# Output stage of a fused recurrence and soft-MoE kernel: eight one-bank PSUM places for both output engines become two one-bank places for ScalarE and three two-bank places for VectorE

## The chip, the cores and the metric

The kernel runs on one core of one Trainium2 chip. The metric is device time in microseconds of one launch; the time before is the median of three runs. A profile is one further execution of the same program, recorded by the hardware profiler. Engines are named as the profile names them: PE is TensorE (PEld its weight loads), DVE is VectorE, ACT is ScalarE, POOL is GpSimd, SP is SyncE, which here issues the output's DMAs.

## The reference, cut to what matters

```python
B, S, D = 4, 5056, 256          # batch, tokens, channels
E, SPE, F = 8, 4, 1024          # experts, slots per expert, hidden size; 32 slots in all

# 1. a gated recurrence along the tokens of each batch
sig = 1 / (1 + exp(-f_logit));  f = lb + (1 - lb) * sig;  i = 1 - f
h[t] = f[t] * h[t-1] + i[t] * x[t]                  # x: [20224, 256] afterwards

# 2. a soft mixture of experts over all 20224 tokens
logits = x @ phi                                    # [20224, 32]
d = softmax(logits, over tokens);  slot_input = d.T @ x     # [32, 256]
slot_out = per expert: relu(slot_input @ w1) @ w2           # [32, 256]
c = softmax(logits, over slots)
out = c @ slot_out                                  # [20224, 256] float32, 20.7 MB
```

Only the last line, the output stage, is touched by the change. It can begin when slot_out is known, which needs all tokens and all experts.

## The kernel before, in words

The first 143 us read f_logit and x (41 MB), run the recurrence and the slot sums, and apply the experts. They leave in SBUF:

- `etall`: exp(logits) of all tokens, the 32 slots of sequence (batch entry) b on partitions 32 b to 32 b + 31;
- `rrow`: the reciprocal of the sum over slots for each token and sequence;
- `slot_out` (L750, VectorE): the experts' output, on the same partitions as `etall`, bf16;
- `slot_bd` (L759, GpSimd, two instructions): the same in two blocks of columns, zero where the sequence is of the other parity, so that one matmul with 64 rows makes the output of two sequences at once.

Just before the output stage, three rows of block 0 of the last sequence are made early: VectorE's L755 and ScalarE's L753 and L756 read `early_ps` out of PSUM, and SP issues them as `total` (L754) and `early` (L757).

The 5056 tokens of a sequence are cut into blocks: blocks 0 and 1 have 16 rows of 128 tokens, the short block (index `end` = 2) has 7 rows, and 64 left-over tokens remain. A row is one matmul into PSUM: 256 columns for one sequence alone (L776, in `share`), 512 columns for a pair of sequences (L828, in `couple`). A vector or scalar instruction then reads it out of PSUM, multiplies by `rrow` and writes the SBUF tile `ob` (one sequence) or `oc` (a pair): `by_vector` (L766) is one VectorE instruction, `by_scalar` (L770) one ScalarE instruction for each 256 columns. When a tile is full, SP issues its DMA: one for a sequence of a block, two for a pair (2 MB each for blocks 0 and 1, 896 KB each for the short block).

PSUM has eight banks of 512 float32 columns. The pool `pout` has eight places of one bank (`bank()`), used by both engines. `next_engine()` gives rows to ScalarE and VectorE in turn. The tile framework places the waits: a matmul into a place waits until the reader of what lay there before is done, and a tile in SBUF waits for the DMA that read its place. Each engine runs its instructions in the order of the program; the order is written out by hand in the last lines of the kernel:

1. `pieces(0, B - 1)`: the remaining 13 rows of block 0 of the last sequence, in five pieces of two to four rows, each with a DMA of its own (L802), VectorE and ScalarE taking a share of each piece;
2. `couple(end, 0)`, `couple(end, 1)`: the short block of all four sequences (L828, L834);
3. `rest()`: the left-over 64 tokens of all sequences, two matmuls (L843), ScalarE copies (L847), VectorE additions and one scaling (L848, L766), two DMAs (L851);
4. `whole(0, B - 2)`: block 0 of sequence 2 alone (L776, L819);
5. `couple(0, 0)`, `couple(1, 0)`, `couple(1, 1)`: what is left of blocks 0 and 1, six DMAs of 2 MB (L834).

Of the kernel before, what the change touches and what calls it, by code (L numbers as in the profile page):

```python
# [9 lines left out]
F32 = mybir.dt.float32  # L10
BF16 = mybir.dt.bfloat16
AX = mybir.AxisListType
ALU = mybir.AluOpType
ACT = mybir.ActivationFunctionType
PSUM = bass.MemoryType.PSUM
# [3 lines left out]
def kernel(  # L19
# [10 lines left out]
    nc = tc.nc  # L30
    B, S, D = x.shape
    E = moe_w1.shape[0]
    F = moe_w1.shape[2]
    NS = moe_phi.shape[1]
    SPE = NS // E
    P = 128
    DC = D // P
    FC = F // P
    R = 4
    G = P * R  # L40
    n_grp = (S + G - 1) // G
# [18 lines left out]
    wide_r = 4 * R  # L60
    n_blk = (S // (P * wide_r))
    blocks = [(i * P * wide_r, wide_r) for i in range(n_blk)]
# [57 lines left out]
    etall = store.tile([P, S + PAD], BF16, name="etall")[:, :S]  # L120
    rrow = store.tile([P, n_grp * R, B], F32, name="rrow")
# [6 lines left out]
    slot_bd = store.tile([P, 2, D], BF16, name="slot_bd")  # L128
# [39 lines left out]
    with tc.tile_pool(name="sp2", bufs=3) as sp2, \  # L168
# [85 lines left out]
        def to_channels(n, ps, t, rest):  # L254
            t = t.bitcast(F32)
            if n // B == odd:
                flat = ps.rearrange("c p r -> c (p r)")
                sides = ident_f.rearrange("p (t u) -> p u t", u=2)
                v = flat[:, ds(0, P * R3)].rearrange("c (p r) -> c p r", r=R3)
                k = P * R3 - n % 2 * L  # L260
                nc.tensor.matmul(flat[:, ds(k, P)], rest.bitcast(F32), sides,
                                 is_transpose=True, start=True, stop=True)
                for r in range(R3):
                    nc.tensor.transpose(v[:, :, r], t[:, r], ident_f)
                return
            for r in range(R):
                nc.tensor.transpose(ps[:, :, r], t[:, r], ident_f)  # L267
# [217 lines left out]
        for n in range(n_unit):  # L485
# [14 lines left out]
            else:  # L500
                end = n >= n_unit - 6
# [97 lines left out]
        for o in range(DC):  # L599
            nc.tensor.matmul(sin_ps[:, o], slot_v[:, o], rep[:, 0],  # L600
                             start=True, stop=True, skip_group_check=True)
# [3 lines left out]
    with tc.tile_pool(name="ew", bufs=1) as ew, \  # L605
# [18 lines left out]
        for q in range(E // Q):  # L624
            hi = ew.tile([P, F], BF16, name=f"hi{q}")
            for k in range(2):
                hi_ps = (psu.tile([P, H], F32, name="hi_ps", tag="up") if q == 0 else
                         pbig.tile([P, H], F32, name="hi_ps", tag=f"hi_ps{k}"))
                for o in range(DC):
                    for j in range(Q):  # L630
                        nc.tensor.matmul(hi_ps[ds(j * NS, NS)], sin[:, o],
                                         w1_sb[q * Q + j][:, o, ds(k * H, H)],
                                         start=(o == 0), stop=(o == DC - 1),
                                         skip_group_check=True)
# [7 lines left out]
        for q in range(E // Q):  # L642
# [4 lines left out]
            if q == 0:  # L647
                nc.tensor.matmul(cs_ps, rep2, cs1, start=True, stop=True)
            k = Q if q == 0 else Q - 1
# [4 lines left out]
            dst = hid[:, :, q * Q, ds(s0, SPE)]  # L654
            dst = bass.AP(tensor=dst.tensor, offset=dst.offset,
                          ap=[list(dst.ap[0]), [(E - 1) * NS, FC], [NS + SPE, k], [1, SPE]])
# [31 lines left out]
        for i in range(n_late):  # L688
# [3 lines left out]
                             start=True, stop=True, skip_group_check=True)  # L692
# [20 lines left out]
        q = n_grp * R - 1  # L713
        for i in range(len(blocks)):
            expert(Q + i)
            row_sums(i)
            if i < len(blocks) - 1:
                spin(so_ps, 3, D)
                k = ds(i * wide_r, wide_r)
# [3 lines left out]
        k = len(blocks) - 1  # L723
# [39 lines left out]
    with tc.tile_pool(name="osb", bufs=3, reuse_waits="tile") as osb:  # L763

        def by_vector(ob, op, scale):
            nc.vector.tensor_tensor(ob, op, scale.broadcast_to(list(ob.shape)), ALU.mult)  # L766

        def by_scalar(ob, op, scale):
            for i in range(ob.shape[1]):
                nc.scalar.activation(ob[:, i], op[:, i], ACT.Copy, scale=scale[:, i])  # L770

        def share(op, i, b, r, k):
            t0, n_r = blocks[i]
            ew = etall[ds(b * NS, NS), ds(t0, P * n_r)].rearrange("s (p r) -> s p r", r=n_r)
            for j in range(k):
                nc.tensor.matmul(op[:, j], ew[:, :, r + j], slot_out[ds(b * NS, NS)],  # L776
                                 start=True, stop=True, skip_group_check=True)

        def scale_of(i, b, r, k):
            return rrow[:, ds(blocks[i][0] // P + r, k), ds(b, 1)]  # L780

        def rows_of(i, b):
            t0, n_r = blocks[i]
            return out[ds(b * S + t0, P * n_r)].rearrange("(p r) d -> p r d", r=n_r)

        pout = ctx.enter_context(
            tc.tile_pool(name="pout", bufs=8, space=PSUM, reuse_waits="tile"))

        def bank():
            return pout.tile([P, 2, D], F32, name="op", tag="op")  # L790

        def pieces(i, b):
            dst = rows_of(i, b)
            ob = osb.tile([P, blocks[i][1], D], F32, name="ob", tag="ob")
            for r, ks in ((3, (1, 1)), (5, (1, 1)), (7, (1, 1)), (9, (2, 2)), (13, (2, 1))):
                q = r
                for k, by in zip(ks, (by_vector, by_scalar)):
                    op = bank()
                    share(op, i, b, q, k)
                    by(ob[:, ds(q, k)], op[:, ds(0, k)], scale_of(i, b, q, k))  # L800
                    q += k
                nc.sync.dma_start(out=dst[:, ds(r, q - r)], in_=ob[:, ds(r, q - r)])  # L802

        turn = [0]

        def next_engine():
            turn[0] += 1
            return turn[0] % 2

        def whole(i, b):  # L810
            n_r = blocks[i][1]
            ob = osb.tile([P, n_r, D], F32, name="ob", tag="ob")
            for r in range(0, n_r, 2):
                k = min(2, n_r - r)
                op = bank()
                share(op, i, b, r, k)
                (by_scalar, by_vector)[next_engine()](
                    ob[:, ds(r, k)], op[:, ds(0, k)], scale_of(i, b, r, k))
            nc.sync.dma_start(out=rows_of(i, b), in_=ob)  # L819

        def couple(i, j):
            t0, n_r = blocks[i]
            ew = etall[ds(j * 2 * NS, 2 * NS), ds(t0, P * n_r)].rearrange(
                "s (p r) -> s p r", r=n_r)
            ob = osb.tile([P, 2, n_r, D], F32, name="oc", tag="oc")
            for r in range(n_r):
                op = bank()
                nc.tensor.matmul(op.rearrange("p u d -> p (u d)"), ew[:, :, r],  # L828
                                 slot_bd[ds(j * 2 * NS, 2 * NS)].rearrange("s u d -> s (u d)"),
                                 start=True, stop=True, skip_group_check=True)  # L830
                (by_scalar, by_vector)[next_engine()](
                    ob[:, :, r], op, rrow[:, t0 // P + r, ds(2 * j, 2)].unsqueeze(2))
            for u in range(2):
                nc.sync.dma_start(out=rows_of(i, 2 * j + u), in_=ob[:, u])  # L834

        def rest():
            n_p = B // 2
            ob = osb.tile([P, n_p, D], F32, name="ob", tag="ob")
            dst = out.rearrange("(b t) d -> t b d", b=B)
            for j in range(n_p):  # L840
                k = ds(j * 2 * NS, 2 * NS)
                op = bank()
                nc.tensor.matmul(op.rearrange("p u d -> p (u d)"),  # L843
                                 left[k].rearrange("s t u -> s (t u)"),
                                 slot_bd[k].rearrange("s u d -> s (u d)"),
                                 start=True, stop=True, skip_group_check=True)
                nc.scalar.copy(ob[:, j], op[:, 0])  # L847
                nc.vector.tensor_tensor(ob[:, j], ob[:, j], op[:, 1], ALU.add)  # L848
            by_vector(ob, ob, rrow[:, n_grp * R - 1, ds(0, n_p)].unsqueeze(2))
            for j in range(n_p):  # L850
                nc.sync.dma_start(out=dst[ds(S - L, L), ds(2 * j, 2)], in_=ob[:, j])  # L851

        pieces(0, B - 1)
        end = len(blocks) - 1
        couple(end, 0)
        couple(end, 1)
        rest()
        whole(0, B - 2)
        for i in range(end):
            for j in range(B // 2):  # L860
                if i or j < B // 2 - 1:
                    couple(i, j)


# [28 lines left out]
```

## Time and profile before

| | us |
|---|---|
| median of 3 runs | 197.69 |
| lowest, highest | 197.34, 197.92 |
| profiled execution, its own time | 197.27 |
| its span, from the first to the last instruction | 195.5 |
| first matmul of the output stage (L776) | 143.47 |
| last PE instruction of the output stage ends | 172.3 |
| last ScalarE instruction ends | 173.6 |

| engine | busy us | share of the span |
|---|---|---|
| PE | 148.4 | 76% |
| DVE | 144.4 | 74% |
| ACT | 141.9 | 73% |
| POOL | 101.8 | 52% |

The span is shorter than the time by what lies around the program (1.8 us here). The shares are means over stages with different limits; the output stage is the last quarter of the span and is read by itself. In the timeline a line gives the start in us, how long the stretch of like instructions took, engine, line of the kernel, operation, what it writes and reads, how many, and in brackets the idle time before it and what ended that. A row like "128x512 f32<-128x512 f32" gives partitions and columns written and read.

### The profile page before, as it was taken

The page shows a single profiled execution, that of the slowest core. Times are in us where ns is not written, and L with a number is a line of the kernel's source. Part 1 is how long each engine was busy: PE and PEld are TensorE (multiplying, and loading weights), DVE is VectorE, ACT ScalarE, POOL GpSimd, SP SyncE. Part 2 cuts the span into 40 slices and gives each one's busy share as a digit, 9 for nine tenths or more (in the row PEclk, how much of TensorE's full clock was granted, in tenths as well). Part 3 has the DMA queues.
Part 4 walks back from the last instruction along what each step waited for, and adds up shares of the span by engine and source line. Part 5 has one row for each costly group of instructions (what it writes and reads, how often), then busy time and mean ns, then how long its engine had stood idle before and what let it go on. Part 6 is the DMA issues. An engine that isn't in the chain of part 4 may idle for free.

```text
span 195.5 us, 3277 instructions
## 1 busy us (share of the span) xinstructions
PE 148.4 (76%) x1202; PEld 104.3 (53%) x1202; DVE 144.4 (74%) x187; ACT 141.9 (73%) x200; POOL 101.8 (52%) x79
## 2 busy tenths in 40 slices
PE   0687599977998979899797987998888999920000
PEld 0476468675776767667585866556664334300000
DVE  2669759989699999999999999544287998920000
ACT  3588686899889999999987799434089999950000
POOL 2689578774998688874969979253030000000000
PEclk9999759996999999999999999999999555555555
DMA  6999999999999999999999999999949999999994
GB/s 212 421 417 417 438 427 419 421 427 370 371 427 426 408 333 419 424 416 335 378 420 422 252 215 214 213 215 214 164 182 417 424 431 429 426 429 429 433 433 211
DMA packets 14305, 70.75 MB, mean 362 GB/s; under 512 B 1601, under 2 KB 2882, under 8 KB 10322
## 3 DMA queue, kind: packets, MB, share of 16 engines
q1 hardware_dynamic: 11520, 62.13, 76.8%
q0 software_dynamic: 2768, 8.42, 21.7%
q8 instruction: 9, 0.15, 0.3%
q14 instruction: 6, 0.05, 0.1%
q10 hardware_dynamic: 2, 0.00, 0.0%
HBM read 58.23 MB, written 20.71 MB: 404 GB/s over the span
## 4 chain that ended last, share of the span: by engine, by line
PE 30%; DMA 20%; DVE 16%; POOL 9%; ACT 7%; issue 5%; SPq 1%; POOLq 1%; ACTq 0%; DVEq 0%
DVE h L319 12%; DMA w_t<-in_moe_w_dram 9%; PE op L828 8%; DMA x_t<-in_x_dram 7%; POOL u_t L252 7%; ACT oc L770 5%; PE hp L332 5%; PE sp L267 4%; PE up L273 4%; DMA f_t<-in_f_logit_dram 4%; DVE ht L351 3%; PE slot_ps L189 2%; PE lg L365 2%; POOL w_sb L147 2%; PE slot_ps L416 1%
## 5 line engine op out<-in xcount | busy, mean ns | idle before, releaser
L252 POOL TENSOR_TENSOR u_t<-s_t,x_t 128x1024 bf16<-128x1024 bf16 (+1 forms) x39 | 82.5, 2131 | 22.8 <-ACT s_t L241 11.9
L319 DVE TENSOR_TENSOR_SCAN h<-a,h,up 128x512 bf16<-128x512 f32 (+1 forms) x72 | 86.8, 1252 | 4.5 <-PE up L273 2.2
L241 ACT ACTIVATE s_t<-f_t 128x2048 bf16<-128x2048 f32 (+2 forms) x23 | 38.3, 1668 | 4.7 <-DMA f_t<-in_f_logit_dram 4.6
L332 PE MATMUL hp<-ident_f,h 128*128 128x128 f32 (+1 forms) x160 | 29.5, 309 | 8.0 <-DVE ht L351 6.7
L332 PEld LDWEIGHTS hp<-ident_f,h 128*128 128x128 f32 (+1 forms) x160 | 23.5, 207 | 19.1 <-DVE ht L351 12.7
L267 PE MATMUL sp<-ident_f,s_t 128*128 128x128 f32 x144 | 22.1, 299 | 6.7 <-ACT s_t L241 4.4
L301 ACT ACTIVATE a<-sp,lbs 128x1024 f32<-128x1024 bf16 x24 | 25.4, 1114 | 1.1 <-PE sp L267 1.0
L770 ACT ACTIVATE oc<-op,rrow 128x256 f32<-128x256 f32 x62 | 24.2, 525 | 0.1
L828 PE MATMUL op<-slot_bd,etall 64*128 64x512 bf16 x62 | 22.5, 570 | 0.7 <-POOL slot_bd L759 0.4
L267 PEld LDWEIGHTS sp<-ident_f,s_t 128*128 128x128 f32 x144 | 18.2, 155 | 8.5 <-ACT s_t L241 4.9
L308 ACT ACTIVATE a<-sp,lbs 128x512 f32<-128x512 bf16 (+2 forms) x22 | 17.8, 857 | 4.7 <-PE sp L267 4.4
L766 DVE TENSOR_TENSOR oc<-op,rrow 128x512 f32<-128x512 f32 x31 | 19.8, 683 | 1.6 <-PE op L828 1.6
L273 PE MATMUL up<-ident_f,u_t 64*128 64x64 f32 x192 | 17.7, 231 | 1.8 <-POOL u_t L252 1.8
L189 PE MATMUL slot_ps<-rep,ident_f 128*128 128x256 f32 x52 | 17.5, 432 | 0.0
L273 PEld LDWEIGHTS up<-ident_f,u_t 64*128 64x128 f32 x192 | 14.1, 139 | 5.6 <-POOL u_t L252 2.1
L828 PEld LDWEIGHTS <-etall 64*128 64x128 bf16 x62 | 9.1, 153 | 13.4 <-issue 8.2
L351 ACT COPY ht<-hp 128x512 f32<-128x512 f32 (+1 forms) x20 | 11.7, 583 | 5.5 <-PE hp L332 5.3
L351 DVE COPY ht<-hp 128x512 f32<-128x512 f32 (+1 forms) x20 | 13.4, 669 | 1.4 <-PE hp L332 1.4
L319 DVE TENSOR_TENSOR_SCAN h<-a,up 128x512 bf16<-128x512 f32 x8 | 9.3, 1208 | 2.6 <-ACT a L308 1.7
L365 PE MATMUL lg<-h,phi 128*32 128x512 bf16 (+1 forms) x80 | 9.8, 412 | 0.3 <-ACT et L389 0.2
L267 PE MATMUL up<-ident_f,u_t 128*128 128x128 f32 x48 | 9.4, 327 | 0.7 <-POOL u_t L252 0.7
L189 PEld LDWEIGHTS slot_ps<-rep,ident_f 128*128 128x128 f32 x52 | 8.5, 199 | 1.8 <-issue 0.8
(132 smaller groups left out, 144.9 us busy)
## 6 DMA issues: line engine op xcount, KB each, us to landing
f_t<-in_f_logit_dram SPq DMA_DIRECT2D x12, 1024.0 KB, 12.0
x_t<-in_x_dram SPq DMA_DIRECT2D x12, 1024.0 KB, 11.5
out_dram<-oc SPq DMA_DIRECT2D x6, 2048.0 KB, 13.7
w_sb<-in_moe_w_dram POOLq DMA_DIRECT2D x14, 512.0 KB, 10.2
f_t<-in_f_logit_dram SPq DMA_DIRECT2D x12, 512.0 KB, 8.4
x_t<-in_x_dram SPq DMA_DIRECT2D x12, 512.0 KB, 9.9
out_dram<-oc SPq DMA_DIRECT2D x4, 896.0 KB, 5.7
out_dram<-ob SPq DMA_DIRECT2D x1, 2048.0 KB, 9.2
```

Source lines behind the costliest of these rows:

```text
L189: nc.tensor.matmul(slot_bank[:, 1], ident_f, wide_rep, start=False, stop=False, skip_group_check=True)
L241: nc.scalar.activation(s_t, f_t, ACT.Sigmoid, scale=-1.0)
L252: nc.gpsimd.tensor_tensor(uts[n][:, :r], s_t[:, :r], x_t[:, :r], ALU.mult)
L267: nc.tensor.transpose(ps[:, :, r], t[:, r], ident_f)
L273: nc.tensor.transpose(v[:, :, r], t(r)[k].bitcast(F32), ident_f[k, k])
L301: nc.scalar.activation(a, sp[:, :, :, :, o], ACT.Identity, scale=nomlb[:, ds(o, 1)], bias=1.0)
L319: nc.vector.tensor_tensor_scan(h[:, :T, o], decays[n // 2, o][:, n % 2, :T], up[:, :T, o], hs[number(g - 1, b)][:, ds(used(g - 1) - 1, 1), ...
L332: nc.tensor.transpose(hp[:n_p, r], hw[:, :n_p, r], ident_f)
L351: copy(hts[g][:n_p, b].rearrange("p r d -> p (r d)").bitcast(F32), hps.pop(n)[:n_p].rearrange("p r c -> p (r c)"))
L766: nc.vector.tensor_tensor(ob, op, scale.broadcast_to(list(ob.shape)), ALU.mult)
L770: nc.scalar.activation(ob[:, i], op[:, i], ACT.Copy, scale=scale[:, i])
L828: nc.tensor.matmul(op.rearrange("p u d -> p (u d)"), ew[:, :, r], slot_bd[ds(j * 2 * NS, 2 * NS)].rearrange("s u d -> s (u d)"), start=Tru ...
```

## The change

The pool gets two kinds of places: `one()`, one bank, two of them, for ScalarE; and `two()`, two banks, three of them, for VectorE, whose instruction now covers up to 1024 columns (four rows of one sequence or two rows of a pair). One `two()` is taken at the start and not used, which shifts the turn of the three. A list of steps takes the place of the strict turn: in a block of 16 rows for a pair the steps are (1, 2, 2, 1, 2) twice, where a 1 is a ScalarE row and a 2 a VectorE instruction over two rows.

The short block's first pair of sequences is no longer made as a pair: `whole(end, 0)` and `whole(end, 1)` make them singly from `slot_out`. The second pair stays a pair. `rest()` is called after `whole(0, B - 2)`, not before it, and its scale is folded into its two kinds of instructions (L862 on ScalarE, L863 on VectorE), so that its third VectorE instruction goes. The line of `by_vector` and `by_scalar` stays L766 and L770, that of the single matmul L776; the pair's matmul is now L783, the pieces' DMA L820, the DMA of `whole` L828, that of `couple` L848, and those of `rest` L866.

```diff
         pout = ctx.enter_context(
-            tc.tile_pool(name="pout", bufs=8, space=PSUM, reuse_waits="tile"))
-        def bank():
-            return pout.tile([P, 2, D], F32, name="op", tag="op")
+            tc.tile_pool(name="pout", bufs=1, space=PSUM, reuse_waits="tile"))
+        def one():
+            return pout.tile([P, 2, D], F32, name="one", tag="one", bufs=2)
+        def two():
+            return pout.tile([P, 2, 2, D], F32, name="two", tag="two", bufs=3)
+        two()
+        def single(ob, i, b, r, k, vector):
+            if vector:
+                op = two().rearrange("p q u d -> p (q u) d")
+            else:
+                op = one()
+            matmuls(op, i, b, r, k)
+            (by_vector if vector else by_scalar)(
+                ob[:, ds(r, k)], op[:, ds(0, k)], scale_of(i, b, r, k))
...
+        def whole(i, b, steps):
+            ob = osb.tile([P, blocks[i][1], D], F32, name="ob", tag="ob")
+            r = 0
+            for k in steps:
+                single(ob, i, b, r, k, k > 2)
+                r += k
             nc.sync.dma_start(out=rows_of(i, b), in_=ob)
...
+            for k in steps:                                  # couple(i, j, steps)
+                scale = rrow[:, ds(t0 // P + r, k), ds(2 * j, 2)]
+                if k == 1:
+                    op = one()
+                    pair_matmul(op, i, j, r)
+                    by_scalar(ob[:, :, r], op, scale[:, 0].unsqueeze(2))
+                else:
+                    op = two()
+                    for q in range(k):
+                        pair_matmul(op[:, q], i, j, r + q)
+                    by_vector(ob[:, :, ds(r, k)].rearrange("p u r d -> p r u d"), op,
+                              scale.unsqueeze(3))
...
-                nc.scalar.copy(ob[:, j], op[:, 0])
-                nc.vector.tensor_tensor(ob[:, j], ob[:, j], op[:, 1], ALU.add)
-            by_vector(ob, ob, rrow[:, n_grp * R - 1, ds(0, n_p)].unsqueeze(2))
+                nc.scalar.activation(ob[:, j], op[:, 0], ACT.Copy, scale=scale)
+                nc.vector.scalar_tensor_tensor(ob[:, j], op[:, 1], scale, ob[:, j],
+                                               ALU.mult, ALU.add)
...
         pieces(0, B - 1)
-        couple(end, 0)
-        couple(end, 1)
+        whole(end, 0, (2, 4, 1))
+        whole(end, 1, (2, 4, 1))
+        couple(end, 1, (1, 2, 1, 2, 1))
+        whole(0, B - 2, (2, 4, 2, 4, 4))
         rest()
-        whole(0, B - 2)
         for i in range(end):
             for j in range(B // 2):
                 if i or j < B // 2 - 1:
-                    couple(i, j)
+                    couple(i, j, (1, 2, 2, 1, 2) * (wide_r // 8))
```

## The prediction

> **What bounds the kernel now.** I read the page first, then windows of the output stage (143 us to the end), then each engine's timeline there, then the DMA issues one by one. The chain of waits names PE L828 and ACT L770, but it starts from the last instruction of an engine, and engines stop at 173.7 us of 195.5. What runs after that is DMA.
>
> ```profile
> PEclk9999759996999999999999999999999555555555
> DMA  6999999999999999999999999999949999999994
> GB/s 212 421 417 417 438 427 419 421 427 370 371 427 426 408 333 419 424 416 335 378 420 422 252 215 214 213 215 214 164 182 417 424 431 429 426 429 429 433 433 211
> ```
>
> One slice is 4.9 us. From slice 31 the DMA engines stay at 9 and 417 to 433 GB/s: 20.7 MB are written between 144.0 and 193.7 us at an even rate, and 1.8 us of closing work follow. So the output stage is one full DMA queue, and an engine's time matters only if a transfer is issued so late that the queue runs dry. The issues:
>
> ```profile
> 143.88 0.34 SPq L757 DMA_DIRECT2D out_dram<-early  x1
> 144.39 2.58 SPq L802 DMA_DIRECT2D out_dram<-ob  x5
> 148.51 4.09 SPq L834 DMA_DIRECT2D out_dram<-oc  x4
> 153.13 2.17 SPq L851 DMA_DIRECT2D out_dram<-ob  x2
> 155.56 1.14 SPq L819 DMA_DIRECT2D out_dram<-ob  x1
> 160.62 14.30 SPq L834 DMA_DIRECT2D out_dram<-oc  x6
> ```
>
> How much room has each? Bytes first move at 144.0, 0.8 us after the first issue (L754 at 143.19); its 128 KB take 0.4 us and land 1.9 us after the issue, so a landing tells 0.5 to 0.7 us late (I take 0.5). A 2 MB transfer takes 4.9 us at 430 GB/s. The transfer of 155.56 lands 9.2 us later and the first of 160.62, couple(0,0)'s, 9.1 us later. The latter needs 0.8 + 4.9 + 0.5 = 6.2 us by itself, so it lay 2.9 us in the queue: the room before couple(0,0) is 2.9 us. In other words the queue would have been empty at 164.3, and an issue after 163.5 leaves it dry. The later couples have twice that room and more. At the front, 'early' (256 KB, 0.7 us at 390 GB/s) keeps the queue busy from 144.7 to 145.5, and the first piece, issued at 144.39, is ready at 145.2: room 0.3 us.
>
> What sets 160.62? These windows are 3.41 us long, on the grid of the clock's changes.
>
> ```profile
> 144.76:148.18 3.42, 2.85 (x15) 1.55 (x14) 3.42 (x7) 3.42 (x10) 0.67 (x1) 1.00 1.05 406
> 148.18:151.59 3.41, 2.65 (x17) 1.71 (x16) 2.06 (x4) 3.41 (x11) 0.00 (x0) 1.00 1.01 416
> 151.59:155.00 3.41, 3.11 (x11) 1.37 (x10) 3.34 (x7) 3.41 (x12) 0.00 (x0) 0.50 1.01 423
> 155.00:158.42 3.42, 3.42 (x9) 1.30 (x8) 3.42 (x7) 3.42 (x11) 0.00 (x0) 0.50 0.99 414
> ```
>
> Columns: PE, PEld, DVE, ACT, POOL busy, granted clock, DMA share, GB/s. TensorE loses half its clock at 151.59 and never regains it, though it is busy all the time. A couple's 512-column matmul then starts every 0.427 us (weight loads at 155.19, 155.61, 156.04), so 16 rows take 6.8 us. With eight banks PE is far ahead: it begins couple(0,0) at 153.04 (timeline), when VectorE begins whole(0,2).
>
> **The change part by part.** Pitches: VectorE 0.60 us for 512 columns (four take 2.48) and 0.335 for 256. For 1024 no row exists. Bounds: two separate 512s, 1.20, and twice the 256-to-512 step on top, 0.60 + 2 x 0.265 = 1.13; I take 1.13, since the step between the two rows is the cost of columns alone. ScalarE: 0.36 for 256 (14 in 5.22). A reader can begin 0.31 us after a full-clock 256-column matmul starts, 0.67 after a half-clock 512 one (160.73 to 161.40). A reader's end frees PE 0.05 later (143.42 to 143.47).
>
> *First place.* The first two-bank place lies on the banks of early_ps[1], which VectorE L755 reads until 143.81. In the built program the first matmul of pieces now waits for that L755, where before it waited for slot_out (L750, ended 143.42). So pieces moves by 0.39 us, from 143.47 to 143.86, and everything on all engines behind it. Of the room of 0.3 about 0.2 us is overdrawn: **+0.2 us**, bounds 0 and 0.4.
>
> *Two places for ScalarE.* The third piece's ScalarE matmul waits for ScalarE's first instruction to end. That costs about 0.1 us per piece, and SP's issues (0.4 to 0.5 us each) still come before the queue empties: nothing by itself, because piece 4's 512 KB and piece 5's 384 KB lie ahead of the short block.
>
> *Short block.* Its first transfer (896 KB) leaves after one sequence instead of after a pair, but at 148.65, not 148.51: PE waits for ScalarE's last piece (146.46), VectorE's 1024-column tile runs 147.40 to 148.54. Room at that point 0.4 us before and after. No gain, since the queue was full there already; no loss.
>
> *Left-over later, and its places.* This is the costly part. rest() now follows whole(0,2). Its two tiles are ScalarE places, read by VectorE too (L863), and VectorE executes in order: that instruction stands behind three 1024-column ones of whole(0,2). The next ScalarE place, couple(0,0)'s first row, waits for it in the built program (VectorE's signal 157, the first L863). Behind that matmul on PE stand all other matmuls. So PE, which before was 2.4 us ahead, stops, VectorE then runs out of tiles, and couple(0,0) begins with empty places.
>
> The schedule, clock half from 148.2 (reasoned below): pieces end 146.6 on VectorE; first sequence's tile ends 148.5; second 150.1; end pair 153.1; whole(0,2) three tiles, 153.7 to 157.2; first L863 ends 157.67 (0.35 + 0.1 for its end). PE then starts couple(0,0) at 157.7, 16 x 0.427 = 6.83, ends at 164.55. The last tile's second matmul starts at 164.12, VectorE begins 0.67 later, 164.8, and ends 1.2 later: issue at about 166.1, against 160.62. The last tile holds both sequences, so the first transfer can't go one instruction ahead as before.
>
> The queue is empty at 164.3 + 0.2 = 164.5; bytes of couple(0,0) come at 166.1 + 0.8 = 166.9: **dry for 2.5 us**. Behind it couple(1,0) comes at 173, room 3 us. So the loss stays and does not grow. Sum at this clock: 0.2 + 2.5 = 2.7, upper with 1.20 a tile 3.2.
>
> *The clock.* In 144.76 to 148.18, which kept the clock, PE ran 12 matmuls of 64 rows x 512 and 2 of 32 x 256. In 148.18 to 151.59, which lost it, 4 of the former and 12 of the latter: 229 thousand row-columns against 410 thousand. After the change the window from 144.76 holds only single sequences, some 19 of 32 x 256, 156 thousand. So the clock should fall one window earlier, near 148.2; where the grid lies in another run is unknown, and any window inside 143.9 to 149.5 has singles alone, so 146.2 to 149.6. By the same schedule this gives +3.3 (146.2) to +2.2 (149.6). I take the middle of the last two, **+2.5**.
>
> The Trainium skill speaks of this in TensorE: Matmul & The Clock Gate, section Part 1: The HAM clock gate: the clock is halved after an idle window of about 3.4 us and is whole again after one busy window. The trace disagrees on both: it fell after a window with PE busy 2.65 of 3.41 us and stayed half through one busy 3.42 of 3.42. By the page's rule couple(0,0) would run at the whole clock, which is a rival below. The page's section A second HAM failure mode: psum-queue depth-cycling says that cycling PSUM banks with short PE pauses degrades matmul throughput; that speaks against this change, and here its price is the early fall.
>
> *Fewer, longer instructions; L862/L863 with the scale folded in.* ScalarE's load falls, VectorE's rises to 6 x 1.13 = 6.8 us per couple, about PE's 6.83. Later couples therefore stay as fast as before and have room. Cover: the DMA queue. If it went, a couple would still cost PE's 6.8.
>
> **Rivals.**
> (a) *Not slower: the room holds.* If VectorE never waited for PE after pieces (ready at 146.6), its work until couple(0,0) is done is 13 x 1.13 + 2 x 0.35 = 15.4, to 162.0: issue before 163.5, and only the 0.2 of the front is lost: 197.9. For it: PE had spare time until 151. Against it: PE's wait on L863 is in the program, and the half clock.
> (b) *Clock whole.* Matmuls every 0.215: the schedule gives couple(0,0) at 164.1, dry 0.6, total +0.8: 198.5. For it: the page's rule. Against it: the rows above.
> (c) *Clock falls at 151.6 as before.* PE starts couple(0,0) at 156.6, issue 165.0, dry 1.4, total +1.6: 199.3.
> (d) *Faster*, the short block fed earlier. The DMA moves bytes from 144.0 to 193.7 without a hole over 0.2 us, so at most the hole at 144.5 and some hand-overs could go, -0.6: 197.1. The same bytes in the same packets speak against it.
>
> **How the numbers follow.** The profiled execution took 197.27 us (span 195.5, 1.8 around it); the median is 197.69, 0.4 above. I add to the median: 197.7 + 2.5 = 200.2. Chances: forecast with its earlier and later falls 0.50; (c) 0.18; (b) 0.14; (a) 0.13; (d) 0.05. A difference under 0.3% (0.6 us) is about what a measurement of this kernel can't tell from none. Slower: 0.50 + 0.18 + 0.14 = 0.82; same 0.13; faster 0.05. The range runs from 197.9, (a), to 201.5 (a fall at 144.8, or 146.2 with 1.20 a tile, +3.8).
>
> **What would show it.** The first L776 at about 143.86, released by DVE early; PEclk half from about 148; an idle PE before couple(0,0)'s first matmul, ended by the first L863, then idle VectorE; the first 2 MB issue of couple(0,0) near 166 with about 6.2 us to landing instead of 9.1; a DMA hole of 2 to 3 us near 165. It is wrong if that transfer is issued before 163.5 or the DMA row shows no hole.

## The result, and the profile after

| | before | after |
|---|---|---|
| median, us | 197.68 | 200.51 |
| lowest, highest | 197.34, 197.92 | 200.16, 200.72 |
| profiled execution, its own time | 197.27 | 200.63 |
| its span | 195.5 | 198.9 |
| last byte of the output moved (trace of the DMA engines) | 193.68 | 197.12 |

Four runs each. The ratio after to before is 1.0143, with a 95% interval from 1.0121 to 1.0164: the change costs 2.8 us. The forecast was 200.2, range 197.9 to 201.5.

Three rows of the page of the changed kernel, in 40 slices of 4.97 us: the granted clock, the DMA engines' busy share, and what they moved.

```profile
PEclk9999889997999999999999999999965555555555
DMA  6999999999999999999999999999499994999996
GB/s 213 416 421 421 433 422 422 425 433 338 404 420 422 380 360 437 422 405 308 409 420 366 234 213 214 213 214 210 71 357 409 435 395 169 448 425 422 422 422 264
```

The output stage, from slice 30 to the end, now has a slice at 169 GB/s and share 4 (number 34, 164 to 169 us) between full ones. Packet by packet, nothing moves from 164.71 to 167.75 us: a hole of 3.04 us. Behind it the queue is as full as before. The hole, a smaller one of 0.09 at 150.14 and a later start (below) make up the 3.44 us by which the last byte is late.

SP's queue in the timeline of the changed kernel (start, length, line, transfer, how many):

```profile
144.03 0.57 SPq L757 DMA_DIRECT2D out_dram<-early  x1
144.93 2.50 SPq L820 DMA_DIRECT2D out_dram<-ob  x5
149.39 1.84 SPq L828 DMA_DIRECT2D out_dram<-ob  x2
153.81 0.84 SPq L848 DMA_DIRECT2D out_dram<-oc  x2
...
166.90 15.22 SPq L848 DMA_DIRECT2D out_dram<-oc  x6
```

couple(0,0)'s first 2 MB leave at 166.90, 6.3 us later than before, and land 6.3 us after the issue, with no time spent in a queue. Why it leaves so late is seen on PE and VectorE. The timeline of PE in the changed kernel, from whole(0,2) on:

```profile
154.57 1.91 PE L776 MATMUL two<-slot_out,etall 32*128 32x256 bf16 x8
156.41 0.61 PE L858 MATMUL one<-slot_bd,left 64*128 64x512 bf16 x2
158.46 0.58 PE L783 MATMUL one<-slot_bd,etall 64*128 64x512 bf16 x1 [1.44 <-DVE ob L863]
158.84 1.91 PE L783 MATMUL two<-slot_bd,etall 64*128 64x512 bf16 x4
```

PE stands still for 1.44 us, and the first L863 (157.93 to 158.41) ends that. And the timeline of VectorE in the changed kernel, with its idle time in brackets:

```profile
144.33 2.44 DVE L766 TENSOR_TENSOR ob<-two,rrow 128x256 f32<-128x256 f32 x5 [0.36 <-PE two L776]
148.10 1.23 DVE L766 TENSOR_TENSOR ob<-two,rrow 128x1024 f32<-128x1024 f32 x1 [1.33 <-PE two L776]
149.61 1.23 DVE L766 TENSOR_TENSOR ob<-two,rrow 128x1024 f32<-128x1024 f32 x1 [0.28 <-PE two L776]
151.24 2.50 DVE L766 TENSOR_TENSOR oc<-two,rrow 128x1024 f32<-128x1024 f32 x2 [0.41 <-PE two L783]
154.44 3.58 DVE L766 TENSOR_TENSOR ob<-two,rrow 128x1024 f32<-128x1024 f32 x3 [0.69 <-PE two L776]
157.93 0.87 DVE L863 SCALAR_TENSOR_TENSOR ob<-one,rrow,ob 128x256 f32<-128x256 f32 x2
159.94 9.18 DVE L766 TENSOR_TENSOR oc<-two,rrow 128x1024 f32<-128x1024 f32 x8 [1.14 <-PE two L783]
```

Between the last piece (146.77) and couple(0,0)'s first tile (159.94) VectorE waits for PE five times, 1.33 + 0.28 + 0.41 + 0.69 + 1.14 = 3.85 us. Only the last of them is the L863 stop; the other four, 2.71 us, come earlier.

The windows of 3.41 us on the grid of the clock in the changed kernel (PE, PEld, DVE, ACT, POOL busy, granted clock, DMA share, GB/s):

```profile
142.53:145.94 3.41, 2.36 (x20) 2.01 (x18) 2.87 (x7) 2.41 (x6) 1.83 (x2) 1.00 0.40 137
145.94:149.36 3.42, 2.84 (x14) 1.76 (x13) 2.05 (x3) 2.88 (x8) 0.00 (x0) 0.50 1.05 416
149.36:152.77 3.41, 3.41 (x9) 0.95 (x7) 2.70 (x3) 2.38 (x6) 0.00 (x0) 0.50 0.96 399
```

The clock falls at 145.94, already at the end of the pieces.

### The profile page after: what moved, and what is told of

It reads as the page before. It is cut to its first block, busy times and chain, and to the rows that moved or that the text cites. A ratio compares the mean times of both kernels' runs of the same rounds, so it can differ in the third digit from the quotient of the medians.

```text
span 198.9 us, 3250 instructions
## 1 busy us (share of the span) xinstructions
PE 153.2 (77%) x1209; PEld 106.4 (54%) x1209; DVE 150.8 (76%) x176; ACT 132.4 (67%) x170; POOL 101.8 (51%) x79
## 4 chain that ended last, share of the span: by engine, by line
DVE 29%; DMA 23%; PE 22%; POOL 7%; issue 5%; ACT 3%; DVEq 1%; SPq 0%; POOLq 0%; ACTq 0%
DMA x_t<-in_x_dram 14%; DVE h L319 13%; DMA w_t<-in_moe_w_dram 9%; DVE oc L766 9%; POOL u_t L252 6%; PE hp L332 4%; PE up L273 3%; DVE ht L351 3%; PE sp L267 3%; PE lg L365 2%; DVE ob L766 2%; POOL w_sb L147 2%; PE slot_ps L189 1%; PE two L776 1%; PE two L783 1%
## 5 line engine op out<-in xcount | busy, mean ns | idle before, releaser
L267 PE MATMUL sp<-ident_f,s_t 128*128 128x128 f32 x144 | 23.1, 308 | 6.1 <-ACT s_t L241 4.4
L766 DVE TENSOR_TENSOR oc<-two,rrow 128x1024 f32<-128x1024 f32 x20 | 23.0, 1217 | 1.6 <-PE two L783 1.5
L267 PEld LDWEIGHTS sp<-ident_f,s_t 128*128 128x128 f32 x144 | 18.7, 158 | 8.1 <-ACT s_t L241 4.9
L770 ACT ACTIVATE oc<-one,rrow 128x256 f32<-128x256 f32 x30 | 12.6, 470 | 11.3 <-PE one L783 11.2
L783 PE MATMUL two<-slot_bd,etall 64*128 64x512 bf16 x40 | 19.2, 628 | 0.1
L189 PE MATMUL slot_ps<-rep,ident_f 128*128 128x256 f32 x52 | 16.8, 418 | 0.0
L783 PEld LDWEIGHTS <-etall 64*128 64x128 bf16 x55 | 8.4, 160 | 15.3 <-issue 12.4
L766 DVE TENSOR_TENSOR ob<-two,rrow 128x1024 f32<-128x1024 f32 (+2 forms) x10 | 8.4, 874 | 2.7 <-PE two L776 2.7
L783 PE MATMUL one<-slot_bd,etall 64*128 64x512 bf16 x15 | 9.2, 629 | 1.4 <-DVE ob L863 1.4
L267 PE MATMUL up<-ident_f,u_t 128*128 128x128 f32 x48 | 9.5, 330 | 0.6 <-POOL u_t L252 0.6
```

Of the source, the lines that this page charges most:

```text
L189: nc.tensor.matmul(slot_bank[:, 1], ident_f, wide_rep, start=False, stop=False, skip_group_check=True)
```

## The experiments

Each kernel ran beside the kernel before on the same chip, whose medians there were 197.66, 197.63 and 197.53 in the three calls.

### The new order with the old places (old_places)

The eight one-bank places, the strict turn of engines and the 512-column instructions of before, with the new order of calls and the first pair made as single sequences:

```diff
         pieces(0, B - 1)
         end = len(blocks) - 1
-        couple(end, 0)
+        whole(end, 0)
+        whole(end, 1)
         couple(end, 1)
+        whole(0, B - 2)
         rest()
-        whole(0, B - 2)
```

> The order of the changed kernel (short block's first two sequences singly, rest() after whole(0,2)) with the eight one-bank places, strict turn and 512-column instructions of the kernel before. My theory (PE loses its lead because only two places are left to ScalarE, one of them held until L863): PE runs ahead again, the first L776 starts 0.05 us after slot_out, couple(0,0)'s first transfer is issued at 160 to 162.7 us, 1 to 3 us before the queue is empty; no hole in the DMA row; 197.7 us (197.2 to 198.2), although the clock still falls at 146 to 150. Rival 1, the late rest() is the cost by itself: 200 us or more. Rival 2, the early fall of the clock is the cost by itself: 199 to 200.5 us, with a hole near 165.

Measured: 197.68 (10 runs), ratio 1.0007 [0.9989, 1.0024]. One window of the trace of old_places, the one in which the changed kernel has its hole:

```profile
164.71:167.75 3.04, 3.04 (x12) 1.23 (x11) 2.55 (x4) 3.00 (x8) 0.00 (x0) 0.50 1.01 431
```

and the same window of the changed kernel:

```profile
164.71:167.75 3.04, 3.04 (x8) 1.14 (x7) 3.04 (x3) 1.60 (x4) 0.00 (x0) 0.50 0.00 0
```

The DMA share is 1.01 against 0.00, and couple(0,0) is issued at 161.09. The clock of old_places fell at 148.46, also one window earlier than before. So the new order, the late left-over tokens, the single sequences and a clock that falls a window earlier cost nothing together. What costs lies in the new places or in the longer instructions, or needs them. In the trace of the changed kernel the clock fell 2.5 us earlier still (145.94), but that date alone does not make the difference: x_onefirst, below, has the new places and a fall at 148.50, and takes 199.95.

### Four places for ScalarE, two for VectorE (places_4_2)

```diff
-            return pout.tile([P, 2, D], F32, name="one", tag="one", bufs=2)
+            return pout.tile([P, 2, D], F32, name="one", tag="one", bufs=4)
-            return pout.tile([P, 2, 2, D], F32, name="two", tag="two", bufs=3)
+            return pout.tile([P, 2, 2, D], F32, name="two", tag="two", bufs=2)
```

> The changed kernel with four one-bank places for ScalarE and two of two banks for VectorE (2 and 3 before), all else as in the changed kernel, rest() and its order included. My theory (PE's lead is limited by ScalarE's places alone, as they stand in PE's order): couple(0,0)'s first place is one that rest() does not hold, PE does not pause for L863; couple(0,0)'s first transfer is issued at 163.2 to 164.0 instead of 166.9, the hole is 0.2 to 0.8 us (1.7 where the clock falls at 146): 198.2 us (197.8 to 199.4). Rival (VectorE's 1024-column instructions or its places set the pace): with one VectorE place less, 200.5 us or more.

Measured: 198.13 (10 runs), ratio 1.0023 [1.0011, 1.0035]; hole 0.79 us. From the timeline of PE in places_4_2:

```profile
155.18 0.61 PE L858 MATMUL one<-slot_bd,left 64*128 64x512 bf16 x2
155.58 0.63 PE L783 MATMUL one<-slot_bd,etall 64*128 64x512 bf16 x1
```

PE goes from the left-over tokens straight into couple(0,0), because its first row no longer needs the place of the first L863. It begins there 2.9 us earlier than in the changed kernel, and 1.2 of these it has already at the left-over tokens (155.18 against 156.41). The instructions of 1024 columns are the same ones, and the issue comes at 164.45 (163.2 to 164.0 was expected). With only the numbers of places changed, 200.51 becomes 198.13: some 2.4 us of the 2.8 go away when ScalarE has four places, though VectorE has one place less. Not all of it need be the places': in this trace the clock fell at 146.78, 0.84 us later than in the changed kernel, and the matmuls of the short block's first VectorE tile took 0.37 us (146.34 to 146.71) instead of 0.85 (147.01 to 147.86). So up to about 0.5 us can be the clock's.

### rest() as the last step (rest_last)

```diff
         whole(0, B - 2, (2, 4, 2, 4, 4))
-        rest()
         for i in range(end):
...
+        rest()
```

> The changed kernel with rest() moved behind the last couple. My theory: couple(0,0)'s first ScalarE place is free as soon as ScalarE has read it, PE does not pause for L863, its first transfer is issued near 164.1 instead of 166.1 to 166.9; the hole shrinks from 3.0 us to between 0.8 and 1.7 us, since two places for ScalarE and the half clock remain: 199.3 us (198.7 to 199.8). Rival 1, the wait on L863 is the whole cost: 197.9 us, no hole over 0.3 us. Rival 2, the clock is the whole cost: 200.5 us, same hole.

Measured: 199.20, ratio 1.0076 [1.0056, 1.0096]; couple(0,0) issued at 165.01 (164.1 was expected), hole 1.72 us. Its PE, in the timeline of rest_last, does not stop before couple(0,0):

```profile
155.74 0.84 PE L776 MATMUL two<-slot_out,etall 32*128 32x256 bf16 x3
156.51 0.64 PE L783 MATMUL one<-slot_bd,etall 64*128 64x512 bf16 x1
156.95 1.91 PE L783 MATMUL two<-slot_bd,etall 64*128 64x512 bf16 x4
```

The issue comes 1.9 us earlier, since the stop at L863 is gone and with it the time of the two L863 themselves (157.93 to 158.80). The hole shrinks by less, 3.04 - 1.72 = 1.3 us, for the 256 KB of the left-over tokens no longer lie ahead of couple(0,0) and the queue is empty 0.6 us sooner (164.11 against 164.71). The rest of the hole, more than half, is there without the stop.

### rest()'s tiles in VectorE's places (rest_in_two)

```diff
-                op = one()
+                op = two()[:, 0]
```

> The changed kernel, in which rest()'s two tiles lie in VectorE's places of two banks, not in ScalarE's of one; order, instructions and DMAs are as they were. Theory 1 (the wait of couple(0,0)'s first ScalarE place for L863 is one part of the stop, ScalarE's two places in the rows before it the other): couple(0,0)'s first matmul starts about 0.8 us earlier, its issue near 166, hole of 2.2 us, 199.7 (199.2 to 200.0). Theory 2 (L863 is all of it): couple(0,0)'s issue before 164, no hole, 197.9. Theory 3 (the wait on L863 has no part; the matmul would be held as long by something else): 200.5 and the issue near 166.9.

Measured: 199.76, ratio 1.0106 [1.0090, 1.0122]; hole 2.22 us. From the timeline of PE in rest_in_two:

```profile
156.47 1.11 PE L858 MATMUL two<-slot_bd,left 64*128 64x512 bf16 x2
157.01 0.65 PE L783 MATMUL one<-slot_bd,etall 64*128 64x512 bf16 x1
158.13 1.86 PE L783 MATMUL two<-slot_bd,etall 64*128 64x512 bf16 x4 [0.48 <-DVE ob L766]
```

couple(0,0)'s first row is free of L863 and starts at 157.01, 1.45 us earlier, but its second matmul waits for a two-bank place, so the issue gains 0.76 (166.14). The matmul gains more than theory 1 said, the issue and the time what it said: the held place is one part only.

### Half the columns in each matmul (half_cols)

From the short block on each matmul moves 128 or 256 columns instead of 256 or 512, so that at the half clock it takes the time of a full one at the whole clock. Each reader takes the same half twice, which its own lines (not shown) arrange, so the kernel leaves out half of the products; readers' sizes, places, order and DMAs stay.

```diff
+            c = ds(0, D if b == B - 1 else D // 2)
...
-                nc.tensor.matmul(op[:, j], ew[:, :, r + j], slot_out[ds(b * NS, NS)],
+                nc.tensor.matmul(op[:, j, c], ew[:, :, r + j], slot_out[ds(b * NS, NS), c],
...
-            nc.tensor.matmul(op.rearrange("p u d -> p (u d)"), ew[:, :, r],
-                             slot_bd[k].rearrange("s u d -> s (u d)"),
+            nc.tensor.matmul(op[:, 0], ew[:, :, r], slot_bd[k, 0],
```

> The changed kernel, in which every matmul from the short block on moves half of its columns (128 instead of 256 for a single sequence, 256 instead of 512 for a pair); readers, places, order and DMAs are as they were, and each reader takes the same half twice, so half of the products is left out. At half a clock a matmul then takes as long as a full one takes at a whole clock. Theory 1 (ScalarE's two places stop PE, and the half clock makes the way from couple(0,0)'s first matmul to its issue longer): PE still waits for the first L863, near 157, but its 16 matmuls take 3.4 us and VectorE sets the rest: couple(0,0) issued near 164.1, hole of 0.6 to 0.8 us, 198.4 (198.0 to 199.1). Theory 2 (the clock has no part in the hole, only the wait has): couple(0,0) issued near 166.9, hole of 3 us, 200.5. Theory 3 (the clock is all of it): no hole, 197.7 to 197.9.

Measured: 197.71 (10 runs), ratio 1.0005 [0.9994, 1.0016]; hole 0.40 us. From the timeline of PE in half_cols:

```profile
153.11 0.89 PE L869 MATMUL one<-slot_bd,left 64*128 64x512 bf16 x2
156.23 0.37 PE L784 MATMUL one<-slot_bd,etall 64*128 64x256 bf16 x1 [2.23 <-DVE ob L874]
```

and of its VectorE:

```profile
155.70 0.86 DVE L874 SCALAR_TENSOR_TENSOR ob<-one,rrow,ob 128x256 f32<-128x256 f32 x2
157.06 9.14 DVE L766 TENSOR_TENSOR oc<-two,rrow 128x1024 f32<-128x1024 f32 x8 [0.49 <-PE two L784]
```

Here PE stops longer at the left-over tokens (2.23 against 1.44 us), and it costs nearly nothing: VectorE waits 0.49 us instead of 1.14 and is the bound from there on, with the issue at 164.00 (164.1 was expected). The time is below what theory 1 gave, 198.4, and in theory 3's range. The clock fell at 145.73 here, so its date is not what helps. So neither the places nor the slow matmuls make the loss alone: with more places the slow matmuls are harmless (old_places, and mended below, where the clock fell at 146.59), and with fast matmuls the two places are. A caveat: half the columns also let a reader begin earlier after a matmul starts, so this is the pace of a whole clock, not a whole clock itself.

### The unused place at the start (x_onefirst)

```diff
-        two()
+        one()
```

> The changed kernel, in which the unused place taken at the start is one of ScalarE's, so that the places lie on other banks and the first L776 waits for ScalarE's early L756 (ended 143.57 in the changed kernel) and slot_out, not for VectorE's L755 (143.97). All else is as it was. Theory 1 (the first wait costs its 0.4 us only while it is not hidden, about 0.2 of them): first L776 at 143.6 to 143.8, 200.3 (200.0 to 200.5), ratio lower by 0.001. Theory 2 (every 0.1 at the front is 0.1 at couple(0,0)'s issue, since the hole's end goes with it and the hole's start does not): couple(0,0) issued near 166.5, 200.1.

Measured: 199.95, ratio 1.0119 [1.0103, 1.0135]. From the timeline of PE in x_onefirst:

```profile
143.76 0.27 PE L776 MATMUL two<-slot_out,etall 32*128 32x256 bf16 x1 [0.56 <-ACT early L756]
...
157.71 0.58 PE L783 MATMUL one<-slot_bd,etall 64*128 64x512 bf16 x1 [1.44 <-DVE ob L863]
```

The front is 0.26 earlier than in the changed kernel (144.02), couple(0,0)'s first matmul 0.75 and its issue 0.76 (166.14). The other 0.5 is the clock's: in this trace it fell at 148.50, not 145.94, so the first matmuls of the short block ran at the whole clock. The gain is some 0.5 us (ratio 1.0119 against 1.0143, with intervals that overlap), where theory 1 gave 0.2 and theory 2 0.4; neither counted on a shift of the clock. That time at the front counts in full at the issue, as theory 2 has it, fits the trace, but the clock moved at the same time. The section on the change says that the unused place shifts the turn of the three; no kernel without it was run, so that is not shown. What this run shows is that the kind taken first decides on which reader the first matmul waits, L756 instead of L755.

### The first pair of the short block as a pair (pair_first)

```diff
-        whole(end, 0, (2, 4, 1))
-        whole(end, 1, (2, 4, 1))
+        couple(end, 0, (1, 2, 1, 2, 1))
```

> The changed kernel with the short block's first two sequences again made as a pair (steps 1, 2, 1, 2, 1), so that 64-row matmuls of 512 columns come in the window from about 145 to 148. My theory (single sequences took the clock one window earlier): the clock falls near 151.6 again or at worst near 149.6; couple(0,0)'s first transfer is issued at 164.4 to 164.9, the first of the short block comes 0.7 us late, holes together 1.1 to 1.6 us: 199.0 us (198.7 to 199.4). Rival (the short block's form does not move the clock, or the clock does not matter): 200.1 to 200.9 us.

Measured: 200.10, ratio 1.0117 [1.0088, 1.0145]. This missed the expected 199.0, for two reasons, and lies where the rival put it (200.1 to 200.9). The clock fell at 145.52, before the first pair began (146.78), so the 64-row matmuls never had a whole clock to hold. And the pair's first transfer waits for both sequences: a window of pair_first shows a DMA share of 0.53, where the changed kernel has 0.94 in the same stretch.

```profile
148.93:152.34 3.41, 3.41 (x10) 1.00 (x7) 3.02 (x3) 2.97 (x8) 0.00 (x0) 0.50 0.53 217
```

The issue comes at 150.88, a hole of 1.60 us at 150.10 and another of 1.54 at 166.05. The single sequences keep the first hole away, but that gains nothing: the two holes together are 3.14 us, and in the changed kernel 0.09 + 3.04 = 3.13, since the bytes held up at 150 keep the queue busy until 166.05 instead of 164.71. Whether pairs would hold the clock stays open, as the run did not test it.

### Holding the clock with more matmuls (fill_128, fill_own, fill_live)

Three kernels wrote extra matmuls into VectorE's places ahead of the real ones, which then overwrite them: fill_128 with 128 rows against the identity, fill_own with the rows of the real matmuls, fill_live with 128 rows of non-zero data and fewer of them.

```diff
+                if r >= 7 or k > 2:
+                    fill(op[:, 0], k)
```

> The changed kernel with matmuls of 128 rows x 256 columns of no use put into VectorE's places ahead of the real ones (one for each real one from the third piece on, four in a tile of four rows, three in a tile of a pair), so that the clock is kept. My theory (the clock goes by rows x columns moved in a window of 3.41 us, about a quarter of the array's time being the limit): PEclk stays whole through couple(0,0); PE still pauses for L863; couple(0,0)'s first transfer is issued at about 164.1, the hole is 0.6 us: 198.5 us (198.0 to 199.0). Rival 1, the clock does not matter to this loss: 200.5 us. Rival 2, the added PE time costs more than the clock gives: over 200.8 us.

> As fill_128, but the matmuls of no use take only the rows of the real ones (32 in a single sequence's tile, 64 in a pair's), so that PE is busy as long and moves as many columns, over fewer rows. My theory (rows count): the clock falls between 146 and 150 us as in the changed kernel, and stays half; a pair's tile of two rows then needs 2 x 0.427 + 3 x 0.213 = 1.5 us of PE, a couple 10.7 us instead of 6.8, so couple(0,0) comes near 170 us and the time is 204 to 206 us. Rival (PE's busy share counts): the clock stays whole as in fill_128 and the time is the same as that one's.

> As fill_128, with operands that are not mostly zero (the slot weights and slot_out, where fill_128 multiplied by the identity) and fewer of them: at most two in a single tile of VectorE's, one in a pair's. Theory 1 (the clock gate goes by what toggles in the array): the clock stays whole through couple(0,0), 198.0 to 199.0 us. Theory 2 (rows and values both do not count, the clock falls after any window with matmuls that do not follow each other closely): PEclk falls between 146 and 151 as before, each pair tile costs 0.21 us more PE at half clock, couple(0,0) comes near 169 us, 202 to 205 us.

Measured: fill_128 217.38 (210.14 to 218.01, so only its sign is read); fill_own 208.95 in its one run; fill_live 208.82 in two runs, ratio 1.0567 [1.0526, 1.0609]. The page of fill_live, its DMA row:

```profile
DMA  6999999999999999999999999994887653999992
```

The clock fell at 147.46, 148.66 and 145.98 and did not come back, so the fills only took PE's time and the DMA engines ran dry in several places. The theories that the clock would be kept missed (fill_128, fill_live). fill_128 came out as its second rival said, that the added PE time costs more than the clock gives; that the clock would fall in fill_own was right, but its time and that of fill_live lie above all that was expected. As tests of the prediction's reason for the fall the three are weak: the lost windows of fill_128 and fill_live were still mostly pieces, whose first rows had no fills. They do show that a busy PE alone doesn't bring the clock back: in fill_128 the window from 154.29 to 157.70 had PE busy throughout and held 311 thousand row-columns (counted from the matmul records), and the clock stayed at half. No window behind the fall, in any of the three, held more than some 360 thousand, less than the 410 thousand that kept the clock in the kernel before.

### Places, order and front mended (mended)

places_4_2, with rest() last and one() taken first; with these places the first matmul of pieces then waits for slot_out alone.

```diff
-        two()
+        one()
...
-        rest()
         for i in range(end):
...
+        rest()
```

> The changed kernel with three parts undone or mended and the short block and long VectorE instructions kept: four places for ScalarE and two for VectorE, rest() behind the last couple, and the banks turned so that the first place waits for slot_out alone. My theory: first L776 at 143.47 plus at most 0.05, couple(0,0)'s first transfer at 162.0 to 162.7 (163.6 where the clock falls at 146), no hole over 0.2 us in most runs: 197.7 us (197.3 to 198.4), same as the kernel before, not faster, since the DMA queue is full throughout. Rival (something else of the change costs, such as the 1024-column instructions): 198.5 us or more with a hole left. Rival 2 (fewer instructions make it faster): under 197.0 us.

Measured: 197.70 (10 runs), ratio 1.0003 [0.9989, 1.0017]. From the timeline of SP in mended:

```profile
163.42 16.05 SPq L848 DMA_DIRECT2D out_dram<-oc  x6
```

The clock fell at 146.59. The issue lies at the edge, 163.42, near the 163.6 expected for such a fall; a hole of 0.55 is left, where at most 0.2 was expected, and the time is that of before. Nothing is gained over it: the queue was full there already.

## Why the prediction came out

**What bounds, and the room.** Right. The queue was empty at 164.71 (forecast 164.5), and the late issue shows as a hole of that length. Behind it couple(1,0) was issued at 173.73 (173 forecast) and no further hole followed.

**The first place.** Right in kind: the first L776 waited for L755, started 0.05 after its end, at 144.02 instead of 143.86, because slot_out itself was 0.16 later in this execution, which is before the change. The DMA engines moved 157 KB less by 146 us than before (windows of half a microsecond), 0.37 us of work, of which 0.16 is slot_out's; the other 0.2 is the term.

**Two places for ScalarE: the step that failed.** The prediction said about 0.1 us per piece and "nothing by itself", and put the loss on the place that L863 holds. rest_last has no such stop and still loses 1.5 us (199.20 against 197.66); places_4_2 keeps rest() where it is and loses 0.5. With two places PE can be only two ScalarE tiles ahead, and since it executes in order, VectorE's matmuls stand behind a ScalarE matmul that waits for ScalarE. In the changed kernel this happens twice, for 0.23 us before 144.96 and here:

```profile
146.63 0.58 PE L776 MATMUL one<-slot_out,etall 32*128 32x256 bf16 x2 [0.58 <-ACT ob L770]
```

From 146.63 until it stops at L863 PE is busy without a break. So VectorE's earlier idle time, 2.71 us, is not waiting for places one by one: it is a start that the places held back by 0.8 us, followed by matmuls at the half clock, which cannot make it good. At the pace of a whole clock it is made good (half_cols: VectorE waits 0.69 us after the pieces, then no more before L874). With four places 0.41 and 0.69 of the 2.71 us remain (places_4_2). The schedule of the prediction carries such waits (its times leave VectorE idle for 0.8 before the first 1024-column tile and 0.6 before whole(0,2)), so the sum had them; what failed was the text's account of where they come from. Had L863's wait been mended alone, as that account suggests, 1.5 us (rest_last) to 2.2 us (rest_in_two, 199.76 against 197.53) would have stayed.

**Left-over later.** Right as a mechanism, line for line: PE idle until the first L863's end, VectorE idle behind it. With the work of L863 this part is worth 1.3 us of the hole, not all of it. The delay against the schedule is there from the short block's first tile, which VectorE ended at 149.33 (148.54 forecast): the clock was half already. The first L863 ended at 158.41 (157.67 forecast), and every later time is late by about as much: PE's start 158.46 (157.7), issue 166.90 (166.1), bytes 167.75 (166.9). From PE's start to the issue it took 8.44 us, forecast 8.4. The 1024-column pitch is 1.14 us (eight in 9.18), near the lower bound of 1.13. The short block neither gained nor lost: its first transfer left at 149.39 (148.65 forecast), with a hole of 0.09.

**The clock.** That it falls earlier was right; when and why were not. It fell at 145.94, just ahead of the 146.2 to 149.6 that the prediction gave, since the lost window began at 142.53 and still held the experts' last matmuls. The range did not follow from its condition either: a window of 3.41 us inside 143.9 to 149.5 ends between 147.3 and 149.5. And the prediction read the output stage alone when it said that the clock stays half through a busy window. Two windows of the changed kernel at the half clock, with PE busy throughout both (columns as above):

```profile
46.96:50.37 3.41, 3.41 (x18) 2.94 (x19) 2.30 (x2) 3.41 (x4) 2.47 (x2) 0.50 1.05 308
152.77:156.18 3.41, 3.41 (x17) 2.48 (x16) 2.72 (x3) 2.41 (x6) 0.00 (x0) 0.50 0.98 410
```

Behind the first the clock is whole again, at 50.37; behind the second it stays half. What differs is the prediction's count of row-columns (rows times columns moved) in the window, 410 thousand against 131 thousand. A float32 matmul counts twice here, since 128 of its columns take 0.109 us at the whole clock (L267) where 256 of bf16 take 0.108 (L776), and a matmul whose weights have 32 columns instead of 128 counts a quarter. Counted so from the matmul records, the windows of all 13 traces from 17 to 170 us, 571 of them, fall in order: behind every one above 410 thousand the clock is whole, behind every one below 360 thousand it is half, and between the two both occur. In the output stage the windows that lost it held 147 to 377 thousand, those ahead of them that kept it 401 thousand or more. No run was made to test this order, so it is an order found in the traces and not a proven rule. The Trainium skill, TensorE: Matmul & The Clock Gate, section A second HAM failure mode: psum-queue depth-cycling, describes a clock that swings to and fro as PE idles shortly between groups in cycled PSUM banks. The traces do not agree for this stage: there the clock falls once and stays down, with two, four or eight places.

**The sum: the clock's date is the mis-sized term.** Profile against profile the change costs 200.63 - 197.27 = 3.36 us: the hole 3.04, and about 0.4 at the front and at 150.1. The prediction's own schedule gives +3.3 for a fall at 146.2, which is what was measured with a fall at 145.94; it took +2.5 for a later one. x_onefirst, with a fall at 148.50, lies 199.88 - 197.27 = 2.6 above before, profile against profile, with a front 0.26 earlier. The medians of before and after differ by 2.83 only, since the profiled execution of before lay 0.41 below its median and that of after 0.12 above. So part of the close hit (200.51 against 200.2) is luck: a term that was too small was added to a median that lay above the profile it was worked out from.

**The rivals.** (a), the room holds, is nearly what half_cols shows once the matmuls are fast: VectorE's work ends within 0.4 us of the point where the queue is empty. (b), the whole clock, was priced at 198.5; the nearest run, half_cols, gives 197.7, so it was probably priced too high; no run had the whole clock itself. (c), the fall at 151.6, did not occur in any run of the new order. (d) has nothing for it: no run was faster than before.

## What to carry to other kernels

Count the places of each reader by what the in-order producer must do ahead of it: a place that is short for one reader stops the matmuls of the other reader as well, and an instruction of both engines (L863) in such a place ties it to the slower queue. Such waits can be harmless at one matmul pace and cost 1.4% at half of it, so price a change of buffers at the pace that the stage really has, and where two causes act together undo each alone. And where a transfer queue is full, look up the room of each transfer first: here 2.9 us decided, and no rearrangement within it gained anything.

## What the runs showed of the hardware

- TensorE's granted clock changes at the edges of a grid of 3.41 us that lies differently in each trace: the last fall comes at 145.5 to 148.7 us in the kernels with the new order, at 151.59 before. In the output stage no later window brought the clock back, though PE was busy for all of many of them; earlier in the changed kernel one did (46.96 to 50.37). The count of row-columns tells the two apart in these traces, with the border between 360 and 410 thousand for a window.
- VectorE's multiply out of PSUM has a pitch of 1.14 us at 1024 columns, hardly less than two of 512 (0.60 each): the long instruction saves 5%, and holds its two banks for 1.23 us where a 512-column one holds one bank for 0.69.
- Extra 256-column matmuls are not free even where PE waits in the trace: the fills of fill_live cost 8 us (208.82 against 200.51).
